# Rows of a head side by side in DRAM, early splits for the output projection, and two moved steps in an attention and MLP kernel

## The chip, the cores and the metric

The kernel runs on one core of one Trainium2 chip. The metric is the device time of one execution in microseconds (us); less is better. Engines are named as in the profile: PE is TensorE, with PEld for its weight loads, DVE is VectorE, ACT is ScalarE, POOL is GpSimd, and SP is SyncE, which here issues nearly all DMAs. An engine works through its instructions in program order; it stops at an instruction whose inputs or whose target buffer are not ready, and whatever stands behind that instruction stops with it.

## The reference

The reference is a transformer layer with layer normalization ahead of each half, in float32, on 2048 rows of 512:

```python
h  = x + A(layernorm(x), wqkv, wo)      # 32 heads of 16, softmax over 2048 keys
h2 = h + B(layernorm(h), w1, w2)        # silu(h @ w1) @ w2, 1792 wide
# A: q, k, v = split(x @ wqkv);  softmax(q @ k.T * 16 ** -0.5) @ v  for each head, then @ wo
# layernorm(x) = (x - mean) / sqrt(var + 1e-5)
```

The output is `h2`, 2048 x 512.

## The kernel before

**Precision.** A float32 operand of a large product is split in two: a high part (a rounded copy, type fp32r) and a low part (what is left, by a subtraction). A product takes three matmuls: high by high, low by high, high by low (`product`, with `mm` at L85). So a tile such as `oh`, `ol` (the high and low part of a 128-row piece of the attention's output `ot`) or `hth`, `htl` (of the turned, normalized rows) needs a copy and a subtraction before the matmuls that read it.

**Queries and keys.** `project_qk` makes 128 rows of q or k (8 heads of 16) for 512 positions, splits them in two 16-bit parts `sh` and `sl`, and stores them in the DRAM tiles `qd` and `kd`, which hold three sets of rows: for k the sets are high, low, high, for q high, high, low, so that one matmul over 48 rows gives all three partial products. `load_k` (L198) and `load_q` (L203) bring a head's 48 rows into the on-chip tiles `ks` and `qs`: 16 rows from each of three places in DRAM that are 512 rows apart. All DMAs stand in one queue on SP (`dma`, L105).

**Work by items.** The 32 heads and 4 blocks of 512 queries make 32 items of four heads each (item `i`: block `i // 8`). An item has 16 groups `c`, one for each 128 keys. In a group, PE makes four score tiles (`ps_s`), ACT takes their exponentials (`pt`, L99), and PE adds the values' products for an earlier group into the bank `pv`. The softmax needs a maximum for each query ahead of its scores: `maximum` (L218) is a matmul over the 48 rows into `ps_m` and a DVE reduction `mx` (L227). Sixty-four of these belong to an item; they are spread over the groups of an earlier item, mostly three or four to a group, by `one_max`, which counts them off. When an item's last maximum is found, `finish_max` folds them to `nm` (on DVE if urgent, on POOL if not) and splits that to `ns` on POOL, and `place_max` (L260) turns `ns` on PE (`ps_n`), copies it out (`mt`), and places it in `qs` by two DMAs.

**Around the end of a block.** An item's sums of exponentials go through DRAM (`sums`, `invert`, `spread`), and `divide` multiplies two items' rows of `ot` by the inverses `den` on POOL; each pair of items fills one of the four 128-column chunks of `ot`, so the last pair of a block fills chunk 3. This goes on while the next block's first item (`FIRSTS`: items 8, 16 and 24) has begun. In that item, at groups 0 to 3 the residual's rows are loaded into `hx`; at group `OUTPUT` = 9 `split_rows` splits row piece 0 on POOL (four chunks at once), at groups 10 to 12 pieces 1 to 3 (the high part on ACT, the low part on POOL), and at groups 10 to 15 `output(b, n)` runs for n = 0 to 5:

```python
project_rows(n)  -> ps_wo (12 matmuls), add_rows: ot <- ps_wo + hx     # n < 4
turn_rows(n - 2): hx turned on PE (ps_tr), hth on ACT, htl on DVE      # 1 < n < 6
found[n] = statistics(row piece n)  (st, mv on DVE, rs on POOL)        # n < 4
normalize(hx[n - 1])                                                   # 0 < n < 5
```

Then `finish_block` runs the MLP of that block (`mlp`): 14 steps `f`, each with the first product (12 matmuls into `ps_w` for f = 0, into the bank `pv` after that), a SiLU on ACT, and the second product of the step before. Bursts of maxima are woven in for the first two blocks and in part for the third. `marks` lists the groups before which an MLP runs; the last block's output and MLP are separate code at the end of the program (`finish_last`).

**Order.** The order on each engine is the order in which the program is written (`keep_in_program_order`). Steps are put off by a count of groups through an agenda (`soon`, `tick`). PSUM banks: in the attention four of kind `st` (scores, `ps_wo`, `ps_tr`, `ps_w`), three of kind `sm` (maxima, `ps_n`), one `pv`. The tiles `oh` and `ol` have two buffers each.

**First phase.** Before item 0 the rows of `x` are normalized and projected, block by block. Block 0's q and k for the first 8 heads are stored, and sixteen loads of 48 rows follow at once in SP's queue; the rows of `x` of block 3 (`load_x(3)`, 1 MB into a `ks` buffer) and the next stores stand behind them.

Of the kernel before, what the change touches and what calls it, by code (L numbers as in the profile page):

```python
# [11 lines left out]
F32R = mybir.dt.float32r  # L12
# [65 lines left out]
def attention_mlp_kernel(ctx: ExitStack, tc: tile.TileContext, x, wqkv, wo, w1, w2, out):  # L78
# [79 lines left out]
    qk_f = nc.scalar.alloc_register("qk_f")  # L158


    qd = dram.tile([3, D, S], F16, name="qd")
    kd = dram.tile([3, D, S], F16, name="kd")

    dn = dram.tile([H, 4, 512], F32, name="dn")
    dr = dram.tile([H, 4, 512], F32, name="dr")
# [29 lines left out]
        qs[i] = vpool.tile([P, 2, 512], F16, name=f"qs{i}")  # L195
    va = vpool.tile([P, KC, H, DH + 1], F32, name="va")

    def load_k(i, k, lo=0, n=S):  # L198
        a, j = HEADS[k]
        h = 4 * (i % 8) + 2 * a + j  # L200
        dma(ks[i % RING][64 * j:64 * j + 48, a, lo:lo + n], kd[:, h * DH:(h + 1) * DH, lo:lo + n])

    def load_q(i, k):  # L203
        a, j = HEADS[k]
        h = 4 * (i % 8) + 2 * a + j
        lo = i // 8 * 512
        dma(qs[i % RING][64 * j:64 * j + 48, a, :], qd[:, h * DH:(h + 1) * DH, lo:lo + 512])

    def fixed_rows(i):
        for j in range(2):  # L210
# [99 lines left out]
    def one_max(half=None, ps=None):  # L310

        i = next_item()
        if i == ITEMS:
            return
        if half is None:
            half = at["half"]
            at["half"] = 1 - half
        if at["blocks"]:

            i = min(range(2), key=lambda n: (todo[n, half] or todo[n, 1 - half] or [(n, KC)])[0][1])  # L320
        elif not todo[i, half] and 64 * (i + 2) <= at["ready"] and KC * i - at["next"] > 12:

            i += 1
        half = half if todo[i, half] else 1 - half
        at["done"] += 1
        found_all = maximum(*todo[i, half].pop(0), ps)

        finish_rest()
        if found_all:
            steps = due_at(i)  # L330
            if at["group"] is None:
                soon(steps, place_max, i)
                finish_max(i, False)
                return
            late.setdefault(at["step"] + steps, []).append(i)
            if steps == WAIT:
                unfinished.append(i)
                found_at["step"] = at["step"]
            else:
                finish_max(i, False)  # L340
# [34 lines left out]
    with ExitStack() as pa:  # L375
# [55 lines left out]
        def project_qk(b, n, beside={}, scale=False, kind="st"):  # L431

            g, key = divmod(n, 2)
            cols = slice(key * D + g * P, key * D + (g + 1) * P)
            ps = bank("ps_qk", kind)
            weave(product(ps, lambda c: wqk_h[:, c, cols], lambda c: wqk_l[:, c, cols],
                          lambda c: xth[b][:, c, :], lambda c: xtl[b][:, c, :], DC),
                  {k: n if callable(n) else (lambda n=n: burst(n)) for k, n in beside.items()})
            sh = xp.tile([P, 512], F16, name="sh")
            sl = xp.tile([P, 512], F16, name="sl", bufs=2)  # L440
            if scale:

                t = scaled[b]
                act("mul", t, ps, qk_s)
                act("copy", sh, t)
                pool("tensor_tensor", sl, t, sh, ALU.subtract)
            else:
                act("mul", sh, ps, qk_s)
                dve("scalar_tensor_tensor", sl, ps, qk_s, sh, op0=ALU.mult, op1=ALU.subtract)
            d = (kd if key else qd)[:, g * P:(g + 1) * P, b * 512:b * 512 + 512]  # L450
            hs, ls = (slice(0, 3, 2), 1) if key else (slice(0, 2), 2)
            dma(d[hs].rearrange("s d n -> d s n"), sh[:, None, :].to_broadcast([P, 2, 512]))
            dma(d[ls], sl)

        def project_v(b, t):
            ps = bank("ps_v")
# [296 lines left out]
                dve("tensor_copy", wh, w)  # L753
            low(wl, w, wh, engine)

    def split_rows(b, t):
        os[t] = [gp.tile([P, DC, P], F32R, name=name) for name in ("oh", "ol")]
        if t:
            act("copy", os[t][0], ot[b % 2][:, t])
        else:  # L760

            pool("tensor_copy", os[t][0], ot[b % 2][:, t])
        low(os[t][1], ot[b % 2][:, t], os[t][0], "pool")

    def split_wo(c, w):
        pool("tensor_copy", wo_h[:, c, :], w)
# [100 lines left out]
    def output(b, n):  # L867

        if n < 4:
            ps = bank("ps_wo")  # L870
            weave(project_rows(n, ps), {6: lambda: burst(3)} if n < MORE[b] else {})
            add_rows(b, n, ps)

        if 1 < n < 6:
            turn_rows(n - 2)
        if n < 4:
            found[n] = statistics(rows_of(b, n))
        if 0 < n < 5:
            normalize(hx[n - 1], rows_of(b, n - 1), *found.pop(n - 1))

    def finish_block(b, pending):

# [159 lines left out]
    for g in range(groups):  # L1042
        tick()
        i, c = divmod(g, KC)
        at["group"], at["next"] = None, g
        if g in marks:
            finish_block(i // 8 - 1, (g - 2, g - 1))
        if i + RING - 1 < ITEMS and 6 <= c < 14:
            (load_k if c % 2 else load_q)(i + RING - 1, c // 2 - 3)
        if g < DC:  # L1050
            w = gp.tile([P, 512], F32, tag="w", name="w", bufs=4)
            dma(w, wo[g * P:(g + 1) * P, :])
            soon(8, split_wo, g, w)
        if i in FIRSTS:
            b, n = i // 8 - 1, c - OUTPUT
            if c < 4:
                load_rows(b, c)
            if c in first_weights:
                load_weights(*first_weights[c])
            if n == 0:  # L1060
                split_rows(b, n)
            if c == 13:
                split_weights("w1", 0, "pool")
        if i == ITEMS - 1:
            if c < 4:
                load_rows(NB - 1, c)
                split_early(c)
            if c == 4:
                for f in range(3):
                    load_weights("w1", f)  # L1070
                load_weights("w2", 0)
                for f in range(2):
                    soon(5, split_weights, "w1", f, "dve", "dve")
        if g == 1:
            dve("memset", pv, 0.0)
        at["group"] = g
        n = maxima(g)

        half = 1 - HEADS[g % 2][1]
        j = next_item()  # L1080
        skip = int(n == 3 and j < ITEMS and len(todo[j, half]) < len(todo[j, 1 - half]))
        for m in range(4):
            k = m ^ (g % 2)
            if (g, k) not in pts:
                scores(g, k)
            if skip <= m < skip + n:
                one_max(1 - HEADS[k][1])
        if found_at["step"] < at["step"]:
            finish_rest()
        for j in late.pop(at["step"], ()):  # L1090

            place_max(j)
        if i in FIRSTS and OUTPUT < c < OUTPUT + 4:

            split_rows(i // 8 - 1, c - OUTPUT)
        if i in FIRSTS and c > OUTPUT:
            output(i // 8 - 1, c - OUTPUT - 1)
        if g - LAG >= 0 and not (g in marks or g - 1 in marks):
            values(g - LAG)
# [34 lines left out]
```

## Time and profile before

| what | value |
|---|---|
| median of 3 runs | 1682.99 us (1679.89 to 1685.68) |
| the profiled execution | 1681.44 us |
| its span | 1679.7 us |
| PE busy | 1657.4 us (99%), 10542 instructions |
| DVE busy | 1449.5 us (86%) |
| ACT busy | 1238.5 us (74%) |
| POOL busy | 397.5 us (24%) |
| granted PE clock, mean | 0.999 |
| longest groups | `mx` reductions on DVE 1258.8 us (x2009), exponentials on ACT 1011.6 us (x2048) |

The shares are means over unlike stages. A busy PE can still wait inside a matmul, and a matmul's end is modelled, so what PE loses is read from the idle time that the rows give in square brackets, with the instruction that ended it, and from the starts of neighbouring rows. In a row of the timeline the columns are the start, the length, the engine, the line and operation, what is written and read, the size and the count of instructions taken together.

### The profile page before, as it was taken

What the parts mean: (1) busy time and instruction counts of PE and PEld (TensorE: products, weight loads), DVE (VectorE), ACT (ScalarE), POOL (GpSimd) and SP (SyncE); (2) the same over time, 40 slices, a digit from 0 to 9 for tenths busy, and PEclk for the clock granted to TensorE, in tenths of its full rate; (3) what the DMA queues carried; (4) which work ended last, traced back from release to release, by engine and by line L of the source; (5) the groups of instructions that cost most, each with busy time, mean ns of one, the idle gap of its engine ahead of it and who ended that gap; (6) DMA issues with size and microseconds to landing.
All of it is one profiled execution on the core that took longest, in us unless ns stands there. A gap on an engine that the chain in (4) does not pass through costs nothing.

```text
span 1679.7 us, 28522 instructions
## 1 busy us (share of the span) xinstructions
PE 1657.4 (99%) x10542; PEld 648.8 (39%) x10542; DVE 1449.5 (86%) x2391; ACT 1238.5 (74%) x2438; POOL 397.5 (24%) x578
## 2 busy tenths in 40 slices
PE   9999999999999999999999999999999999999999
PEld 7666422222245532222245532222245542222387
DVE  7899999999978889999978889999978889997343
ACT  5323699999952279999953279999962379999743
POOL 5323411211244301211144311211135311211100
PEclk9999999999999999999999999999999999999999
DMA  5434311111222111111223111111222211100222
GB/s 181 115 92 145 115 44 36 40 49 36 62 64 85 58 49 32 37 52 37 60 62 89 60 50 31 37 47 40 62 63 79 69 50 32 35 12 21 64 76 81
DMA packets 100763, 102.82 MB, mean 61 GB/s; under 512 B 19092, under 2 KB 77524, under 8 KB 100624
## 3 DMA queue, kind: packets, MB, share of 16 engines
q1 hardware_dynamic: 100624, 101.01, 20.6%
q8 instruction: 82, 1.34, 0.3%
q14 instruction: 57, 0.47, 0.1%
HBM read 77.72 MB, written 17.29 MB: 57 GB/s over the span
## 4 chain that ended last, share of the span: by engine, by line
PE 86%; ACT 5%; DVE 4%; DMA 2%; POOL 1%; issue 1%; SPq 1%; DVEq 0%; POOLq 0%
PE pv L85 33%; PE ps_s L85 19%; PE ps_m L85 10%; PE ps_acc L85 10%; PE ps_qk L85 5%; ACT pt L99 5%; PE ps_wo L85 3%; PE ps_w L85 3%; PE ps_v L85 3%; DVE mx L227 2%; PE ps_tr L88 1%; SPq L105 1%; DMA ks<-in_A_x_dram 1%; POOL ri L92 1%; DVE pvs L102 0%
## 5 line engine op out<-in xcount | busy, mean ns | idle before, releaser
L227 DVE TENSOR_REDUCE mx<-ps_m 128x1 f32<-128x512 f32 x2009 | 1258.8, 684 | 89.0 <-PE ps_m L85 61.5
L99 ACT ACTIVATE pt<-ps_s 128x512 f32<-128x512 f32 x2048 | 1011.6, 609 | 36.1 <-PE ps_m L85 22.8
L85 PE MATMUL pv<-pt,va 128*17 128x512 f32 x4096 | 537.5, 598 | 1.7 <-DVE pv L102 0.5
L85 PE MATMUL ps_s<-qs,ks 64*128 64x512 f16 x2048 | 531.1, 379 | 3.1 <-ACT pt L99 1.7
L85 PE MATMUL ps_m<-ks,qs 48*128 48x512 f16 x2009 | 502.6, 380 | 3.3 <-DVE mx L227 3.3
L85 PEld LDWEIGHTS <-ks 64*128 64x128 f16 x2048 | 148.7, 95 | 546.7 <-issue 435.4
L92 POOL TENSOR_TENSOR ri<-rc,minus 128x16 f32<-128x16 f32 x31 | 90.7, 2924 | 339.3 <-DMA rc<-dn 339.3
L85 PEld LDWEIGHTS pv<-pt,va 128*17 128x17 f32 x4096 | 68.9, 95 | 218.0 <-issue 203.5
L85 PEld LDWEIGHTS <-qs 48*128 48x128 f16 x2048 | 117.7, 94 | 70.0 <-issue 63.9
L99 ACT CAST w2h<-w 128x512 fp32r<-128x512 f32 x56 | 34.7, 620 | 102.3 <-PE ps_acc L85 102.3
L99 ACT ACTIVATE g<-pv 128x512 f32<-128x512 f32 x39 | 23.3, 597 | 102.8 <-PE pv L85 102.8
L85 PE MATMUL ps_acc<-w2l,gh 128*128 128x512 f32 x224 | 92.9, 415 | 0.0
L85 PE MATMUL ps_acc<-w2h,gh 128*128 128x512 f32 x224 | 92.4, 413 | 0.0
L92 POOL TENSOR_TENSOR w2l<-w,w2h 128x512 fp32r<-128x512 f32 x42 | 53.8, 1282 | 153.4 <-ACT w2h L99 153.4
L85 PE MATMUL ps_acc<-w2h,gl 128*128 128x512 f32 x224 | 88.1, 393 | 0.0
L102 DVE TENSOR_TENSOR gl<-g,gh 128x512 fp32r<-128x512 f32 x53 | 37.2, 701 | 46.7 <-ACT gh L99 46.7
L99 ACT ACTIVATE ks<-ps_qk,qk_s 128x512 f32<-128x512 f32 x30 | 20.7, 690 | 72.3 <-PE ps_qk L85 65.7
L85 PE MATMUL pv<-htl,w1h 128*128 128x512 f32 x156 | 65.6, 420 | 0.0
L85 PE MATMUL pv<-hth,w1h 128*128 128x512 f32 x156 | 62.5, 401 | 0.0
L85 PE MATMUL pv<-hth,w1l 128*128 128x512 f32 x156 | 61.4, 393 | 0.0
L92 POOL TENSOR_TENSOR w1l<-w,w1h 128x512 fp32r<-128x512 f32 x42 | 54.3, 1292 | 10.8 <-ACT w1h L99 10.8
L92 POOL TENSOR_SCALAR nm<-nm 128x16 f32<-128x16 f32 x51 | 13.0, 255 | 183.7 <-DVE nm L237 180.3
(135 smaller groups left out, 1395.8 us busy)
## 6 DMA issues: line engine op xcount, KB each, us to landing
w<-in_B_w_dram SPq DMA_DIRECT2D x112, 256.0 KB
ks<-kd SPq DMA_DIRECT2D x120, 192.0 KB
qs<-qd SPq DMA_DIRECT2D x128, 48.0 KB
kd<-sh SPq DMA_DIRECT2D x16, 256.0 KB
qd<-sh SPq DMA_DIRECT2D x16, 256.0 KB
hx<-in_A_x_dram SPq DMA_DIRECT2D x16, 256.0 KB
ot<-pvs SPq DMA_DIRECT2D x124, 32.0 KB
den<-dr SPq DMA_DIRECT2D x124, 32.0 KB
```

Of the source, the lines that this page charges most:

```text
L85: tc.keep_in_program_order(nc.tensor.matmul(*a, **k))
L88: tc.keep_in_program_order(nc.tensor.transpose(*a))
L92: tc.keep_in_program_order(getattr(nc.gpsimd, op)(*a, **k))
L99: pin(getattr(nc.scalar, fn)(*a, **k))
L102: pin(getattr(nc.vector, fn)(*a, **k))
L105: pin(nc.sync.dma_start(*a))
L227: pin(nc.vector.tensor_reduce(mx[i][:, j, a, qt, kb:kb + 1], ps, axis=AX.X, op=ALU.max))
```

## The change

There are four edits.

1. **Layout.** `qd` and `kd` become `[D, 3, S]`: the three rows that belong to one of the 512 columns lie next to each other, and a head's 48 rows are adjacent. `rows_of_head` gives them as 48 rows; the loads' source pattern changes from three runs of 16 rows to one run of 48. The stores write the same 1 KB pieces, each to a place three rows further on than the last.
2. **The end of the maxima ahead of an MLP.** When an item's last maximum is found in the group just before a mark, `finish_max` is called at once with the urgent form and `place_max` is put on the agenda; before, the item went through the list of unfinished ones. This concerns the items finished there ahead of the first two blocks' MLPs.
3. **Early splits.** Row pieces 0 and 1 are split in two steps: chunks 0 to 2 at groups 3 and 4 and chunk 3 at group 9, all on POOL. The high part of piece 1 moves from ACT to POOL. Pieces 2 and 3 are split as before.
4. **Normalization.** In `output`, `normalize(hx[n - 1])` is written ahead of `turn_rows(n - 2)` and `statistics` of piece n.

```diff
-    qd = dram.tile([3, D, S], F16, name="qd")
-    kd = dram.tile([3, D, S], F16, name="kd")
+    qd = dram.tile([D, 3, S], F16, name="qd")
+    kd = dram.tile([D, 3, S], F16, name="kd")
...
+    def rows_of_head(t, h):
+        return t[h * DH:(h + 1) * DH].rearrange("d s n -> (d s) n")
+
     def load_k(i, k, lo=0, n=S):
...
-        dma(ks[i % RING][64 * j:64 * j + 48, a, lo:lo + n], kd[:, h * DH:(h + 1) * DH, lo:lo + n])
+        dma(ks[i % RING][64 * j:64 * j + 48, a, lo:lo + n], rows_of_head(kd, h)[:, lo:lo + n])
...
-        dma(qs[i % RING][64 * j:64 * j + 48, a, :], qd[:, h * DH:(h + 1) * DH, lo:lo + 512])
+        dma(qs[i % RING][64 * j:64 * j + 48, a, :], rows_of_head(qd, h)[:, lo:lo + 512])
...
         if found_all:
             steps = due_at(i)
-            if at["group"] is None:
+            g = at["group"]
+            if g is None or g + 1 in marks:
                 soon(steps, place_max, i)
-                finish_max(i, False)
+                finish_max(i, g is not None)
                 return
...
-            d = (kd if key else qd)[:, g * P:(g + 1) * P, b * 512:b * 512 + 512]
+            d = (kd if key else qd)[g * P:(g + 1) * P, :, b * 512:b * 512 + 512]
             hs, ls = (slice(0, 3, 2), 1) if key else (slice(0, 2), 2)
-            dma(d[hs].rearrange("s d n -> d s n"), sh[:, None, :].to_broadcast([P, 2, 512]))
-            dma(d[ls], sl)
+            dma(d[:, hs], sh[:, None, :].to_broadcast([P, 2, 512]))
+            dma(d[:, ls], sl)
...
-    def split_rows(b, t):
-        os[t] = [gp.tile([P, DC, P], F32R, name=name) for name in ("oh", "ol")]
-        if t:
-            act("copy", os[t][0], ot[b % 2][:, t])
+    def split_rows(b, t, chunks=slice(None)):
+        if chunks.start != DC - 1:
+            os[t] = [gp.tile([P, DC, P], F32R, name=name) for name in ("oh", "ol")]
+        (h, l), o = (x[:, chunks] for x in os[t]), ot[b % 2][:, t, chunks]
+        if t > 1:
+            act("copy", h, o)
         else:
 
-            pool("tensor_copy", os[t][0], ot[b % 2][:, t])
-        low(os[t][1], ot[b % 2][:, t], os[t][0], "pool")
+            pool("tensor_copy", h, o)
+        low(l, o, h, "pool")
...
             add_rows(b, n, ps)
+        if 0 < n < 5:
+            normalize(hx[n - 1], rows_of(b, n - 1), *found.pop(n - 1))
 
         if 1 < n < 6:
             turn_rows(n - 2)
         if n < 4:
             found[n] = statistics(rows_of(b, n))
-        if 0 < n < 5:
-            normalize(hx[n - 1], rows_of(b, n - 1), *found.pop(n - 1))
...
+            if c in (3, 4):
+
+                split_rows(b, c - 3, slice(0, DC - 1))
             if n == 0:
-                split_rows(b, n)
+                for t in range(2):
+                    split_rows(b, t, slice(DC - 1, DC))
...
-        if i in FIRSTS and OUTPUT < c < OUTPUT + 4:
+        if i in FIRSTS and OUTPUT + 1 < c < OUTPUT + 4:
 
             split_rows(i // 8 - 1, c - OUTPUT)
```

What stands on POOL at the end of block 0 before the change (`ri`, `rc`: the inversion of the last item's sums; `den`: the divide of chunk 3):

```order
L92 TENSOR_TENSOR ns<-nm,ns 128x2x8
L92 TENSOR_TENSOR ri<-rc,minus 128x16
L92 TENSOR_TENSOR rc<-rc,ri 128x16
L92 TENSOR_SCALAR rc<-rc 128x16
L92 TENSOR_TENSOR ri<-ri,rc 128x16
L92 TENSOR_TENSOR ot_2191<-ot_2191,den 128x4x128
L92 CAST oh<-ot_2191 128x512
L92 TENSOR_TENSOR ol<-ot_2191,oh 128x512 x2
```

The same place on POOL with the change:

```order
L92 CAST oh<-ot_2191 128x384
L92 TENSOR_TENSOR ol<-ot_2191,oh 128x384
L92 CAST oh<-ot_2191 128x384
L92 TENSOR_TENSOR ol<-ot_2191,oh 128x384
L92 TENSOR_TENSOR ri<-rc,minus 128x16
L92 TENSOR_TENSOR rc<-rc,ri 128x16
L92 TENSOR_SCALAR rc<-rc 128x16
L92 TENSOR_TENSOR ri<-ri,rc 128x16
L92 TENSOR_TENSOR ot_2191<-ot_2191,den 128x4x128
L92 CAST oh<-ot_2191 128x128
L92 TENSOR_TENSOR ol<-ot_2191,oh 128x128
L92 CAST oh<-ot_2191 128x128
```

Three quarters of two pieces now stand ahead of the inversion and the divide, and a quarter of each behind it; the second `ol` of 128 x 128 follows in the next row.

DVE in the output of block 0 before the change, at n = 2 (`mx` rows are maxima of the group):

```order
L102 TENSOR_TENSOR ot_2191<-ps_wo,hx 128x512
L102 TENSOR_TENSOR htl<-ps_tr,hth 128x4x128
L102 BN_STATS st<-ot_2191 128x6
L102 BN_AGGR mv<-st 128x2
L102 TENSOR_SCALAR hx<-ot_2191,mv,rs 128x512
L227 TENSOR_REDUCE mx<-ps_m 128x1 x3
```

And with the change (the reductions' line has become L231):

```order
L102 TENSOR_TENSOR ot_2191<-ps_wo,hx 128x512
L102 TENSOR_SCALAR hx<-ot_2191,mv,rs 128x512
L102 TENSOR_TENSOR htl<-ps_tr,hth 128x4x128
L102 BN_STATS st<-ot_2191 128x6
L102 BN_AGGR mv<-st 128x2
L231 TENSOR_REDUCE mx<-ps_m 128x1 x3
```

The normalization `hx` has moved ahead of the low part `htl` and the statistics.

PE at the head of step f = 1 of block 0's MLP before the change (`ps_n` turns the maxima's `ns`):

```order
L85 LDWEIGHTS qs_90
L85 MATMUL ps_m<-ks_89,qs_90 128x512
L88 LDWEIGHTS ns
L88 MATMUL ps_n<-ident_h,ns 32x128
L85 MATMUL pv<-hth,w1h 128x512
L85 MATMUL pv<-hth,w1l 128x512
```

And PE at the head of step f = 0 with the change, where `ps_n` now stands:

```order
L88 MATMUL ps_tr<-ident,hx 128x128 x4
L85 MATMUL pv<-pt,va 17x512 x12
L88 LDWEIGHTS ns
L88 MATMUL ps_n<-ident_h,ns 32x128
L85 MATMUL ps_w_6837<-hth,w1h 128x512
L85 MATMUL ps_w_6837<-hth,w1l 128x512
```

The transpose has moved from behind the maxima of step 0 to ahead of that step's first product; otherwise PE has the same instructions in the same order.

## The prediction

> **What bounds the kernel now.** I read the page first: PE is busy 99% of the span. That says little, since a waiting exponential also keeps PE's stream slow without an idle row. So I cut the program into its stages with the table of stretches. Columns: the stretch, its length, busy PE (and instructions), PEld, DVE, ACT, POOL, the granted clock, the DMA share, GB/s.
>
> ```profile
> 80.00:130.00 50.00, 49.75 (x237) 31.37 (x236) 48.57 (x81) 13.68 (x23) 13.53 (x19) 1.00 0.34 91
> 196.00:462.00 266.00, 265.46 (x2021) 59.27 (x2021) 254.04 (x414) 265.54 (x541) 49.22 (x80) 1.00 0.18 49
> 462.00:494.00 32.00, 29.91 (x178) 13.89 (x175) 25.40 (x46) 18.64 (x36) 11.80 (x18) 1.00 0.25 71
> 494.00:606.00 112.00, 111.07 (x488) 64.56 (x486) 94.95 (x154) 39.36 (x68) 43.40 (x50) 1.00 0.21 62
> ```
>
> In the attention (196 to 462) ACT is busy 265.54 of 266.00 us: the exponentials set the pace there, and nothing that the change does on PE, DVE or POOL in that stretch is worth anything as long as it doesn't make ACT wait. In the output stage (462 to 494) ACT is busy 18.64 of 32 and PE idles 2.09; in the MLP (494 to 606) PE sets the pace. In the first phase PE and DVE are both nearly full (49.75 and 48.57 of 50). A wait of PE in the output stage, which comes three times, or in the MLP or the first phase, delays everything behind it. Next I read what PE waits for, over the whole run (total us, times, longest).
>
> ```profile
> PE ps_m L85 <- DVE mx L227: 3.3, 7, 1.3
> PE ps_wo L85 <- POOL ol L92: 2.5, 3, 0.9
> PE ps_tr L88 <- DVE hx L102: 2.3, 3, 0.8
> PE ps_wo L85 <- POOL oh L92: 0.9, 1, 0.9
> ```
>
> Three of these four rows lie in the output stages, once or so in each of the three blocks, and name the steps that the change touches. They are all small: the whole change plays for some 10 us of 1681.
>
> **Early splits.** This is the timeline at the first output, and below it the rows of the second and third.
>
> ```profile
> 462.36 0.61 POOL L92 CAST oh<-ot 128x512 fp32r<-128x512 f32 x1
> 463.03 0.50 PE L85 MATMUL ps_wo<-wo_h,oh 128*128 128x512 f32 x1
> 463.06 1.27 POOL L92 TENSOR_TENSOR ol<-ot,oh 128x512 fp32r<-128x512 f32 x1
> 464.38 0.50 PE L85 MATMUL ps_wo<-wo_h,ol 128*128 128x512 f32 x1 [0.84 <-POOL ol L92]
> 464.72 0.40 PE L85 MATMUL ps_wo<-wo_l,oh 128*128 128x512 f32 x1
> 464.95 0.39 PE L85 MATMUL ps_wo<-wo_h,oh 128*128 128x512 f32 x1
> ```
>
> ```profile
> 838.77 5.99 ACT L99 ACTIVATE pt<-ps_s 128x512 f32<-128x512 f32 x12
> 844.25 0.50 PE L85 MATMUL ps_wo<-wo_h,oh 128*128 128x512 f32 x1 [0.94 <-POOL oh L92]
> 845.61 0.50 PE L85 MATMUL ps_wo<-wo_h,ol 128*128 128x512 f32 x1 [0.85 <-POOL ol L92]
> 1226.04 0.50 PE L85 MATMUL ps_wo<-wo_h,ol 128*128 128x512 f32 x1 [0.78 <-POOL ol L92]
> ```
>
> Matmuls of this product follow each other by 0.23 us (464.72 to 464.95). The second starts 464.38 - 463.03 = 1.35 after the first, so 1.12 is lost; in the second block 845.61 - 844.25 = 1.36, so 1.13; the third block's idle time is 0.06 less than the first's, so 1.05. Sum 3.3. With the change, chunk 0 of `oh` and `ol` is ready five groups before, and chunk 3 is needed by the tenth matmul, 9 x 0.23 = 2.1 us after the first. POOL's work between is a quarter of each: cover even if it cost the full 0.61 + 1.27 = 1.88. If that cover failed, the wait would come back at chunk 3.
>
> The first matmul also waited, in the second block 0.94 for `oh`. What is late next is its bank, which one of the group's four exponentials must free. Exponentials follow by (5.99 - 0.61) / 11 = 0.49 with 0.61 for one; this run of twelve ends at 844.76, so the first of its last four ends at 844.76 - 3 x 0.49 = 843.29, before PE is free for it at 844.25 - 0.94 = 843.31. So 0.9 goes. In the other blocks no such wait is recorded, and I count 0.1 for both. Early splits: 3.3 + 0.9 + 0.1 = **4.3** (3.3 if the second block's first wait finds another cause, 4.9 if the first matmul of each block gains 0.3 more).
>
> The early splits themselves lie in the attention, where POOL is busy 49.22 of 266 and ACT doesn't wait for POOL; in full size a piece takes 0.61 + 1.27 = 1.88, so two pieces take under 3.8 us of POOL in two groups of 4 x 0.49 = 1.96. The inversion of sums is queued behind them on POOL; it comes later in the program and the divide of chunk 3 later still, so a delay of some tenths there would show as a later `oh` at 462.36. I count nothing. Nor do I for piece 1's copy that leaves ACT, since ACT waits for PE in the output stage.
>
> **Normalization.** The rows of the first block at n = 2:
>
> ```profile
> 485.37 0.69 DVE L102 TENSOR_TENSOR htl<-ps_tr,hth 128x512 fp32r<-128x512 f32 x1 [0.30 <-ACT hth L99]
> 486.05 2.07 ACT L99 ACTIVATE pt<-ps_s 128x512 f32<-128x512 f32 x4 [0.72 <-PE ps_m L85]
> 486.79 0.52 DVE L102 TENSOR_SCALAR hx<-ot,mv,rs 128x512 f32<-128x512 f32 x1
> 487.45 0.63 PE L88 MATMUL ps_tr<-ident,hx 128*128 128x128 f32 x4 [0.78 <-DVE hx L102]
> 488.12 0.59 ACT L99 CAST hth<-ps_tr 128x512 fp32r<-128x512 f32 x1
> 489.42 1.57 ACT L99 ACTIVATE pt<-ps_s 128x512 f32<-128x512 f32 x3 [0.72 <-PE ps_m L85]
> 490.07 0.37 PE L85 MATMUL ps_s<-qs,ks 64*128 64x512 f16 x1 [0.25 <-ACT pt L99]
> 490.37 0.44 PE L88 MATMUL ps_tr<-ident,hx 128*128 128x128 f32 x2
> ```
>
> With `hx` ahead of `htl` and the statistics, it ends about 1.5 us sooner, and the wait of 0.78 goes. It doesn't all come through. What is late next is the bank of `ps_tr`: the first exponential of the group ends at 486.05 + 0.61 = 486.66, so the transposes start near 486.72, 0.73 sooner. PE then goes on to the next scores, whose exponentials start at 488.71 instead of 489.42: the copy `hth` keeps its place behind four exponentials, at 488.12 to 488.71, which is just in time. The scores at 490.07 wait for an exponential and so gain the same, but the next transposes (490.37) then wait for the bank of a later exponential, which I put at 489.87: 0.5 of the 0.7 is left. Three blocks: **1.5** (2.3 if the whole wait goes; 0 if the bank or the exponentials take all). The price is a later `htl`: it now stands behind 0.52 of `hx`, but DVE idled 0.30 ahead of it, so it is 0.2 later, and a group's length lies between it and the MLP. I count nothing for it.
>
> **The transpose of the maxima.** Before, PE at the heads of steps 1 and 0:
>
> ```profile
> 497.97 0.37 PE L85 MATMUL ps_m<-ks,qs 48*128 48x512 f16 x1 [0.20 <-DVE mx L227]
> 498.57 0.22 PE L88 MATMUL ps_n<-ident_h,ns 128*32 128x128 f16 x1 [0.23 <-DVE mx L227]
> 498.71 0.50 PE L85 MATMUL pv<-hth,w1h 128*128 128x512 f32 x1
> 492.81 0.22 POOL L92 TENSOR_TENSOR ns<-nm,ns 128x16 f16<-128x16 f32 x1
> 493.66 0.50 PE L85 MATMUL ps_w<-hth,w1h 128*128 128x512 f32 x1
> ```
>
> The transpose waited for a bank that a maximum's reduction frees. Without it, the product's first matmul would follow the maximum by 0.23, at 498.20 rather than 498.71: 0.5 gained. At its new place it costs its own slot, 498.71 - 498.57 = 0.14; its `ns` is ready at 493.03, before PE comes there at 493.66. So 0.35 in each of two blocks: **0.7** (0 to 1.0). The fold of the maxima on DVE comes one maximum earlier, and the copy `mt` and two DMAs on SP go with the transpose, one step sooner; nobody waits for them there. The third block has no such transpose.
>
> **Layout.** The trace doesn't show the new pattern, so this term is the least sure. The rows are SP's last of sixteen loads, the load of `x` behind them, DVE's wait for that, four maxima on PE and what follows, a wait for a load at the end of the first phase, a store-free stretch of the attention with only loads in flight, and a DMA whose two sides are spread otherwise.
>
> ```profile
> 43.34 0.67 SPq L105 DMA_DIRECT2D ks<-kd  x1
> 46.27 0.39 SPq L105 DMA_DIRECT2D ks<-in_A_x_dram  x1
> 54.48 0.69 DVE L102 BATCH_NORM_STATS2 st<-ks 128x6 f32<-128x512 f32 x1 [2.60 <-DMA ks<-in_A_x_dram]
> 55.95 0.39 PE L85 MATMUL ps_m<-ks,qs 48*128 48x512 f16 x1
> 57.61 0.37 PE L85 MATMUL ps_m<-ks,qs 48*128 48x512 f16 x1 [1.27 <-DVE mx L227]
> 59.11 1.08 PE L88 MATMUL ps_tr<-ident,ks 128*128 128x128 f32 x4
> 133.05 0.09 PEld L85 LDWEIGHTS <-qs 48*128 48x128 f16 x1 [1.38 <-DMA qs<-qd]
> 616.00:618.00 2.00, 2.00 (x18) 0.44 (x15) 1.93 (x4) 2.00 (x5) 0.00 (x0) 1.00 0.19 74
> 56.62 0.73 SPq L105 DMA_DIRECT2D qs<-fix_q  x1
> ```
>
> Loads alone keep a share of 0.19 of 16 engines busy: 3.0 engines, as many as the source has runs. So a load's packets queue on three engines, and the transfers of `x`, which need all, wait there too. The Trainium skill, page "DMA: Bandwidth & Descriptors", section "Why a DMA increments its semaphore by 16 and not by 1", says that the number of engines is the largest one up to 16 that divides the slowest dimension of both patterns: 3 before, which the 0.19 bears out, and 16 for 48 rows, which no run here shows yet. By that rule the sum below stands; with three engines as now it would be the first rival's. I take from the row alone that a pattern with 48 in the place of 3 spreads wider.
>
> DVE waits 2.60 for `x` at 54.48, and its reductions come late by as much: PE runs the four maxima from 55.95 to 59.11, 3.16 us, where four matmuls without a wait, 0.23 apart, would leave it after some 0.8. So up to 2.4 goes if `x` lands 2.6 sooner. SP issues it no sooner (46.27, after sixteen loads), only its way is free: I take the whole 2.4, since 8.2 us from issue to use is long for a transfer that shares three full engines. At 133.05 a weight load waits 1.38 for a load of queries, of which PE's last matmul (0.39) covers a part: PE loses about 1.0, and that load gets faster. The stores move the same pieces to places further apart; no row shows such a store, and the lower end allows for its cost. Sum **3.4** (0 to 4.5).
>
> **Sum.** 4.3 + 1.5 + 0.7 + 3.4 = 9.9. Against the profiled execution, 1681.4: **1671.5**. The median of the runs, 1682.99, lies 1.6 higher, by which it would be 1673.1; I keep the first and let the range hold the second. By upper ends 4.9 + 2.3 + 1.0 + 4.5 = 12.7: 1668.7.
>
> **The rivals.**
> - *The loads gain nothing on the path.* Either the layout does not spread the packets, or DVE, full for 48.57 of 50 us behind that place, eats what PE gains. Against: DVE too starts 2.6 sooner. Left is 4.3 + 1.5 + 0.7 = 6.5: 1675. Chance 0.20.
> - *The output stages keep their length.* Exponentials and banks pace the groups there too: each row with 0.72 at ACT's start shows ACT waiting for PE and not the other way, which speaks against. Only 3.4 is left: 1678. Chance 0.10.
> - *Slower: SP's price for a load.* A load holds SP's queue 0.67 us now, a fill with a 16-row pattern 0.73. If 48 separate rows cost more to write out, the sixteen loads ahead of `x` delay it by 16 times the surplus. At twice the price that is 16 x 0.67 = 10.7 later at DVE's wait; the layout's 3.4 is lost, and the total is 1681.4 - 6.5 + 10.7 = 1685.6. It decides from a surplus of 6.5 / 16 = 0.41 on. The 0.73 is far below that. Chance 0.07.
> - *Nothing moves*: the gains of all parts are taken up before the next attention's first exponential, 1681. Against: ACT idles in all these stages, so nothing there takes them up. Chance 0.05.
>
> **How the numbers follow.** The forecast has 0.58. A measurement can tell about 0.3%, 5 us, from no change. Faster by more: the forecast, and 0.18 of the first rival's 0.20 (6.5 is near the bound) = 0.76. Within: 0.02 + 0.10 + 0.05 = 0.17. Slower: 0.07. The range goes from the upper ends less the runs' scatter (1682.99 - 1679.89 = 2.9), 1665.8, to the second rival from the median's side, 1678.0 + 1.6 = 1679.6; it leaves out the slower case, that of nothing, and a part of the others' scatter.
>
> **What would show it.** Right: no wait of `ps_wo` for POOL, the stretch of 32.00 us at the output about 2 shorter; `ps_tr` waiting for an exponential and not for `hx`; `ps_n` in PE's row ahead of the first `ps_w`; the share of 0.19 in load-only stretches spread over more engines, a shorter wait at DVE for `x`, SP's load still near 0.7. Wrong: a load above 1.0 on SP, a wait for `x` that is still there, a new wait of PE for `htl` at the MLP's head, or a wait for `oh` at chunk 3.

## The result and the profile after

| | before | after |
|---|---|---|
| median of 6 runs each | 1681.08 us | 1670.37 us |
| lowest to highest | 1679.89 to 1685.68 | 1670.20 to 1670.89 |
| span of the profiled execution | 1679.7 | 1668.4 |

The ratio is 0.9932, with a 95% interval of 0.992 to 0.9945. By medians the change is worth 10.7 us, by the two profiled spans 11.3. The scatter fell too, from 5.8 us to 0.7. Of the kernels tested below, four had one run each of 2356 to 8553 us, which the ratios and ranges leave out and the medians count as one run of twelve. Where the time came from is read from the starts of the same instructions in both traces, since PE has the same instructions in the same order but for the place of one transpose in each of the first two blocks:

| instruction | before | after | difference | new here |
|---|---|---|---|---|
| `ps_v` behind DVE's wait for `x` | 62.54 | 58.50 | -4.04 | 4.04 |
| `ps_m` behind the load of queries | 133.05 | 128.15 | -4.90 | 0.86 |
| a `pv` shortly ahead of the first output | 455.00 | 450.35 | -4.65 | -0.25 |
| block 1: third matmul of `ps_wo` | 464.72 | 458.91 | -5.81 | 1.16 |
| block 1: `ps_tr` at n = 3 | 490.37 | 484.02 | -6.35 | 0.54 |
| block 1: `pv` at the head of step 1 | 498.71 | 491.97 | -6.74 | 0.39 |
| block 2: third matmul of `ps_wo` | 845.94 | 837.24 | -8.70 | 1.96 |
| block 2: `ps_tr` at n = 3 | 871.58 | 862.35 | -9.23 | 0.53 |
| block 2: `pv` at the head of step 1 | 879.92 | 870.31 | -9.61 | 0.38 |
| block 3: third matmul of `ps_wo` | 1226.37 | 1215.71 | -10.66 | 1.05 |
| block 3: `ps_tr` at n = 3 | 1250.55 | 1239.35 | -11.20 | 0.54 |

So in this pair of profiles the layout gave 4.65, the early splits 1.16 + 1.96 + 1.05 = 4.17, the normalization 1.61 and the transpose of the maxima 0.77: 11.2 of the 11.3. The waits of PE after the change, whole run:

```profile
PE ps_s L85 <- ACT pt L99: 1.6, 5, 0.5
PE ps_i L88 <- POOL ident masks.py:199: 1.5, 1, 1.5
PE ps_m L85 <- DVE mx L231: 0.7, 3, 0.3
PE ps_n L88 <- DVE mx L231: 0.6, 4, 0.2
```

The three rows that the prediction was made from, `ps_wo` for `ol` and `oh` and `ps_tr` for `hx`, are gone, and `ps_m` for `mx` fell from 3.3 to 0.7. At the first output, timeline after:

```profile
458.37 0.47 PE L85 MATMUL ps_wo<-wo_h,oh 128*128 128x512 f32 x1
458.68 0.40 PE L85 MATMUL ps_wo<-wo_h,ol 128*128 128x512 f32 x1
459.42 0.46 POOL L92 TENSOR_TENSOR ol<-ot,oh 128x128 fp32r<-128x128 f32 x1
480.88 0.42 PEld L88 LDWEIGHTS ps_tr<-ident,hx 128*128 128x128 f32 x4 [0.53 <-ACT pt L99]
484.02 0.42 PEld L88 LDWEIGHTS ps_tr<-ident,hx 128*128 128x128 f32 x4 [0.98 <-ACT pt L99]
487.19 0.22 PE L88 MATMUL ps_n<-ident_h,ns 128*32 128x128 f16 x1
487.34 0.51 PE L85 MATMUL ps_w<-hth,w1h 128*128 128x512 f32 x1
```

The second matmul follows the first by 0.31, and chunk 3 of `ol` is ready at 459.42 + 0.46 = 459.88, ahead of the tenth matmul, which starts at 461.26 behind three maxima. The transposes now wait for an exponential, that is, for their bank. `ps_n` takes 0.15 ahead of the MLP's first matmul. In the first phase, SP's last load, the load of `x`, and what waited for it (timeline after):

```profile
38.89 0.43 SPq L105 DMA_DIRECT2D ks<-kd  x1
40.39 0.41 SPq L105 DMA_DIRECT2D ks<-in_A_x_dram  x1
51.93 0.68 DVE L102 BATCH_NORM_STATS2 st<-ks 128x6 f32<-128x512 f32 x1
56.08 0.61 PE L85 MATMUL ps_m<-ks,qs 48*128 48x512 f16 x4
```

A load holds SP for 0.43 and not for 0.67, so `x` is issued 5.9 us sooner; DVE's wait of 2.60 is gone, and the four maxima stand in one row. The loads at the start of an attention, in stretches of 1 us after:

```profile
606.00:607.00 1.00, 1.00 (x12) 0.21 (x6) 1.00 (x2) 1.00 (x3) 0.00 (x0) 1.00 0.97 224
608.00:609.00 1.00, 1.00 (x12) 0.21 (x6) 0.98 (x2) 1.00 (x3) 0.00 (x0) 1.00 0.42 81
609.00:610.00 1.00, 1.00 (x9) 0.23 (x9) 0.95 (x2) 1.00 (x4) 0.00 (x0) 1.00 0.04 12
```

The DMA share there is 0.97 and soon 0.04, where it was 0.19 before: all sixteen engines for a short time. This is what the rule from the Trainium skill, page "DMA: Bandwidth & Descriptors", named in the prediction gives for 48 rows.

One thing in the trace of before had not been seen ahead of the result. PE's matmuls behind the wait for `x` followed each other by 0.42 and not by 0.23 (stretches of 2 us, before; the clock is the third value from the right):

```profile
56.00:58.00 2.00, 0.71 (x3) 0.14 (x3) 1.77 (x4) 0.00 (x0) 1.92 (x4) 1.00 0.20 67
58.00:60.00 2.00, 1.57 (x7) 0.99 (x7) 1.97 (x5) 1.31 (x2) 0.50 (x1) 0.80 0.68 125
60.00:62.00 2.00, 2.00 (x6) 1.62 (x6) 1.97 (x6) 0.59 (x1) 1.58 (x4) 0.50 0.83 122
62.00:64.00 2.00, 2.00 (x8) 1.33 (x7) 2.00 (x4) 0.00 (x0) 2.00 (x3) 0.85 0.84 99
```

The granted clock fell to 0.50 behind a stretch in which PE was busy 0.71 of 2 us. The wait took 2.5 us, and the slow matmuls behind it took another 1.5.

### The profile page after: what moved, and what is told of

Its sections match the earlier page's. It is cut to its first block, busy times and chain, and to the rows that moved or that the text cites. A ratio compares the mean times of both kernels' runs of the same rounds, so it can differ in the third digit from the quotient of the medians.

```text
span 1668.4 us, 28544 instructions
## 1 busy us (share of the span) xinstructions
PE 1655.0 (99%) x10542; PEld 648.1 (39%) x10542; DVE 1448.6 (87%) x2391; ACT 1236.4 (74%) x2435; POOL 399.0 (24%) x593
## 4 chain that ended last, share of the span: by engine, by line
PE 89%; ACT 5%; DVE 4%; issue 1%; DMA 1%; POOL 0%; SPq 0%; DVEq 0%; POOLq 0%
PE pv L85 34%; PE ps_s L85 20%; PE ps_m L85 11%; PE ps_acc L85 10%; PE ps_qk L85 5%; ACT pt L99 5%; PE ps_wo L85 3%; PE ps_w L85 3%; PE ps_v L85 3%; DVE mx L231 2%; PE ps_tr L88 1%; DVE pvs L102 0%; PE ps_n L88 0%; DVE st L102 0%; SPq L105 0%
## 5 line engine op out<-in xcount | busy, mean ns | idle before, releaser
L231 DVE TENSOR_REDUCE mx<-ps_m 128x1 f32<-128x512 f32 x2009 | 1258.8, 684 | 83.3 <-PE ps_m L85 55.7
L92 POOL TENSOR_TENSOR mx<-mx 128x32 f32<-128x32 f32 x38 | 9.5, 250 | 199.1 <-DVE mx L231 197.5
```

Of the source, the lines that this page charges most:

```text
L92: tc.keep_in_program_order(getattr(nc.gpsimd, op)(*a, **k))
L231: pin(nc.vector.tensor_reduce(mx[i][:, j, a, qt, kb:kb + 1], ps, axis=AX.X, op=ALU.max))
```

## The experiments

The theory was that the parts act at separate places and add up, and that a wait can cost more than its length by the clock. The rivals were that the parts help or hide each other, and that a wait costs its length. All ratios are to the kernel before, run on the same chip. The three groups of kernels below ran on three different chips, so a kernel of one group is compared with one of another by its ratio.

### Each part alone

The edits are the four parts of the diff above, each put into the kernel before.

> The layout alone (part 1), nothing else changed. Theory (the parts act at separate places and add up): the whole gain of the first phase comes from here, so the first exponential starts 4.6 us earlier than in the kernel before and the time is 4.7 us less (ratio 0.9972); the output stages keep all their waits (ps_wo for POOL 3.4 in all, ps_tr for hx 2.3). Rival (the parts help each other, so that a part alone is worth less): under 3.5 us less.

> The early splits alone (part 3). Theory: 4.1 us less (1.1, 2.0 and 1.0 in the three blocks), all of it at the first and second matmul of ps_wo; the first phase as before. Rival (the gain at ps_wo is taken back by the later wait of ps_tr for hx, which stays here): 2 us less or none, with a longer wait of ps_tr for hx than 2.3 in all.

> The normalization's place alone (part 4). Theory: ps_tr no longer waits for hx, 0.75 gained at n = 2 of each block and 0.2 given back at n = 3 by a wait for an exponential: 1.6 us less in all (ratio 0.999). Rival (ACT's exponentials pace the group, so that nothing is left of it at the MLP): 0 to 0.3 us less.

> The maxima's transpose ahead of the MLP alone (part 2). Theory: 0.4 us at the head of step 1 of the first two MLPs, 0.8 us less in all, too little for the times but plain in the trace. Rival (at its new place the transpose costs what it saves, or the MLP's second step waits for DVE instead): 0.

| part alone | median | ratio (95%) | runs, lowest to highest |
|---|---|---|---|
| before | 1681.64 | | 1678.62 to 1686.52 |
| layout | 1676.63 | 0.9970 (0.9959 to 0.9982) | 1676.23 to 1677.22 |
| early splits | 1675.71 | 0.9969 (0.9956 to 0.9981) | 1674.55 to 1681.37 |
| normalization | 1680.19 | 0.9997 (0.9986 to 1.0008) | 1677.95 to 1688.58 |
| maxima's transpose | 1680.52 | 0.9991 (0.9980 to 1.0003) | 1678.44 to 1684.26 |

The four sum to 0.30 + 0.31 + 0.03 + 0.09 = 0.73%, against 0.68% for the whole: within the intervals, each some 0.12% to either side, they add up. With the layout alone the first exponential starts at 180.91 and not at 185.11, 4.2 sooner where 4.6 was expected, and the output keeps its waits, 3.4 for POOL and 2.3 for `hx`. With the early splits alone the waits for POOL are gone and that for `hx` is still 2.3, so the rival there fell. The last two are too small for the times alone; their traces show the same steps as the whole change: with the normalization alone `ps_tr` at n = 2 comes 0.75 sooner and 0.21 is lost again at n = 3, and with the transpose alone the head of step 1 comes 0.38 sooner.

The three kernels without the layout have the first phase of the kernel before, instruction for instruction, and yet DVE's wait for `x` differs (timelines of the early splits, of the normalization and of the transpose alone):

```profile
52.72 0.69 DVE L102 BATCH_NORM_STATS2 st<-ks 128x6 f32<-128x512 f32 x1 [0.82 <-DMA ks<-in_A_x_dram]
```
```profile
53.72 0.70 DVE L102 BATCH_NORM_STATS2 st<-ks 128x6 f32<-128x512 f32 x1 [1.55 <-DMA ks<-in_A_x_dram]
```
```profile
53.44 0.69 DVE L102 BATCH_NORM_STATS2 st<-ks 128x6 f32<-128x512 f32 x1 [0.63 <-DMA ks<-in_A_x_dram]
```

0.82, 1.55 and 0.63, against 2.60 in the profiled execution before: the wait is a matter of the execution, and the 4.65 of the table above is one draw of it. In these three the first exponential starts at 182.40, 183.38 and 183.24, against 185.11 before and 180.47 with the whole change: measured from them, the layout's first phase is worth 1.9 to 2.9. The 5.0 that the layout alone gains by medians seems to hold more than this phase. In none of these three did the clock fall there. It fell elsewhere, in the kernel with the transpose alone, at the second block's output (stretches of 2 us):

```profile
842.00:844.00 2.00, 1.03 (x2) 0.69 (x3) 0.35 (x1) 0.99 (x3) 1.92 (x3) 0.82 0.24 65
844.00:846.00 2.00, 2.00 (x7) 1.11 (x6) 0.00 (x0) 0.00 (x0) 0.64 (x1) 0.50 0.54 168
```

That wait for `oh` and `ol` is in the kernel before as well, where the clock stayed at 1.00. So what the early splits take away also cost more than its length in some executions, which may be why they alone gave 5.9 by medians and 4.2 by the starts. The mean granted clock of each run points the same way. Of the 27 runs of the kernel before in this group, eight have 0.997 or 0.998 and took 1682.0 to 1686.5; the other nineteen have 0.999 or 1.000 and took 1678.6 to 1683.5. All runs of the layout alone and of the early splits alone have 0.999 or 1.000.

### What in the layout counts

In the kernel before, only the order of a load's rows: 16 runs of 3, DRAM as it was (and the same for q):

```diff
-        dma(ks[i % RING][64 * j:64 * j + 48, a, lo:lo + n], kd[:, h * DH:(h + 1) * DH, lo:lo + n])
+        dma(ks[i % RING][64 * j:64 * j + 48, a, lo:lo + n], kd[:, h * DH:(h + 1) * DH, lo:lo + n].rearrange("s d n -> d s n"))
```

> The kernel before with its old layout (three sets 512 rows apart); only the order in which a load names its 48 rows is changed, so that its source has 16 runs of 3 rows and not 3 runs of 16 (q and k alike, so the products are the same). Theory A (what counts is over how many DMA engines a load is spread): all of the layout's 4.7 us comes, although no rows are adjacent, and the share of load-only stretches is spread wider. Theory B (what counts is SP's time for a load, 0.67 before and 0.42 after): SP still takes about 0.67, since the pattern still has three levels, and x is issued as late as before: under 1.5 us less. Theory C (what counts is that the rows are adjacent): nothing.

In the changed kernel, the adjacent rows named in 3 runs:

```diff
-        return t[h * DH:(h + 1) * DH].rearrange("d s n -> (d s) n")
+        return t[h * DH:(h + 1) * DH].rearrange("d s n -> s d n")
```

> The changed kernel, but each load names its 48 adjacent rows in 3 runs of 16 rows (every third row). Theory A (engines): the load goes over 3 engines again, and the layout's 4.7 us are lost: about 1675. Theory B (SP's time): SP takes 0.67 again, and most of the 4.7 us is lost as well. Theory C (adjacent rows): nothing is lost, 1670.4.

In the kernel before, `x` ahead of the second eight loads:

```diff
                         for i in range(2):
+                            if b == 0 and i == 1:
+                                load_x(3)
...
-                if b == 1 and n == 0:
-                    load_x(3)
```

> The kernel before, with the 1 MB load of x for the last block issued behind the first eight of the sixteen loads instead of behind all and two stores; layout as before. It takes the wait of DVE for x away by an earlier issue alone. Theory (the wait for x is worth 3.6 us: 2.5 of waiting and about 1.1 of a lower clock after it): 3 to 3.6 us less by the time of the next projections, if the second eight loads, now later, do not hold the first maxima up. Rival (DVE's own work paces this stretch): under 1 us less.

| kernel | median | ratio (95%) | SP for a load | DVE's wait for `x` | `ps_m` behind the load of queries |
|---|---|---|---|---|---|
| before | 1681.31 | | 0.67 | 2.60 | 133.05 |
| before, 16 runs of 3 | 1679.31 | 0.9983 (0.9973 to 0.9994) | 0.59 | none | 128.06 |
| changed, 3 runs of 16 | 1673.04 | 0.9949 (0.9930 to 0.9967) | 0.68 | 0.28 | 129.74 |
| before, `x` sooner | 1680.40 | 0.9993 (0.9980 to 1.0006) | 0.67 | none | |

The load-only stretches of the two kernels, first with 16 runs, then with 3 runs of adjacent rows:

```profile
609.00:610.00 1.00, 1.00 (x11) 0.13 (x8) 1.00 (x3) 1.00 (x3) 0.00 (x0) 1.00 0.80 183
613.00:614.00 1.00, 1.00 (x9) 0.13 (x8) 1.00 (x3) 1.00 (x3) 0.00 (x0) 1.00 0.19 68
```

The 16 runs reach a share of 0.80, the 3 runs stay at the 0.19 of the kernel before. With 16 runs and no adjacent rows the first phase is that of the changed kernel, 133.05 to 128.06: adjacency is not needed there. With adjacent rows in 3 runs, the kernel is slower than the changed one by 0.17% in the ratios, 2.9 us, though the intervals overlap; its span is 1.8 longer. That is less than the 4.7 of theory A. PE waits for the queries again:

```profile
129.74 0.39 PE L85 MATMUL ps_m<-ks,qs 48*128 48x512 f16 x1 [0.97 <-DMA qs<-qd]
```

So the spread over the engines is what the layout does for that wait (theory A; B and C fall there: SP's time with 16 runs was nearer the old, 0.59, and the whole gain came). For the wait for `x` these profiles do not tell the spread from an earlier issue. A load of `x` issued 7.7 us sooner behind slow loads, at 38.54, had none, and PE stood 3.6 us earlier from there to 175 us; but 3 runs with an issue at 44.80 had only 0.28, and the wait moves by some 2 us without any edit. In the median of the kernel with `x` sooner little of the 3.6 is left, 0.9 us, with an interval that holds zero. Five of its twelve runs have a mean clock of 0.996 to 0.998, so a part may have gone to a lower clock elsewhere; where is not shown.

The kernel with 16 runs has the first phase's gain, but its median is 2.0 less than before and not the 4.7 of theory A: by the ratios 2.2 slower than the layout alone, with intervals that overlap, and by the two spans 2.2 as well. In the profile the outputs hold the difference (timeline and stretches):

```profile
458.43 0.49 PE L85 MATMUL ps_wo<-wo_h,oh 128*128 128x512 f32 x1 [0.41 <-POOL oh L92]
459.78 0.52 PE L85 MATMUL ps_wo<-wo_h,ol 128*128 128x512 f32 x1 [0.85 <-POOL ol L92]
460.95 0.63 PE L85 MATMUL ps_wo<-wo_h,ol 128*128 128x512 f32 x1
```
```profile
460.00:462.00 2.00, 2.00 (x7) 1.12 (x7) 0.00 (x0) 0.00 (x0) 1.27 (x1) 0.53 1.06 217
842.00:844.00 2.00, 1.89 (x5) 1.28 (x5) 0.00 (x0) 0.16 (x1) 1.33 (x2) 0.61 1.08 221
```

Behind waits of 0.41 and 0.85 the clock fell to 0.53, in the second block, behind 0.54 and 0.85, to 0.61 and then 0.54. Against the layout alone PE loses 1.6 from the first output's start to its end and 1.5 in the second: more than the 2.2 between the two spans. With the layout alone PE waited there for `ol` only, 0.79, but in the second block as long as in the kernel before, and the clock stayed. Why it fell here is open.

### Whether the clock is the cause

> The kernel before, with six transposes of the identity (work of no use) on PE behind the first of the four maxima that wait for DVE and x, so that PE is busy in a part of its wait; the wait itself stays. Theory (a wait of that length lowers PE's granted clock, which costs another 1.1 to 1.4 us after it): granted clock near 1.0 in the 5 us behind the wait, and about 1 us less in the trace. Rival (the matmuls behind the wait are slow for another reason, such as the DMA load of that stretch): the clock row and the pitch of 0.42 stay, 0 us.

The edit puts `idle(6)` behind the first of four maxima:

```diff
+                    if b == 2 and n == 0:
+                        burst(1)
+                        idle(6)
+                        n_max -= 1
```

It tells nothing on this, for two reasons that the timeline shows:

```profile
52.97 0.39 PE L85 MATMUL ps_m<-ks,qs 48*128 48x512 f16 x1
53.29 0.87 PE L88 MATMUL ps_i<-ident 128*128 128x128 f32 x6
57.58 0.61 PE L85 MATMUL ps_m<-ks,qs 48*128 48x512 f16 x4
```

The transposes stand one group of maxima too early: the maxima in which PE waited before, from 55.95 on, are those at 57.58 here. And `x` came in time, so there was no wait to fill. The median was 1684.09 (ratio 1.0017, 1.0003 to 1.003), 2.8 more than before, which six transposes of 0.87 together do not explain; where the runs lose it is open. One such loss shows in the trace, a wait for the rows that `place_max` puts in `qs`, at the start of an item:

```profile
442.70 0.60 PE L85 MATMUL ps_s<-qs,ks 64*128 64x512 f16 x1 [2.63 <-DMA qs<-mt]
```
```profile
442.00:444.00 2.00, 1.29 (x7) 0.43 (x7) 0.62 (x2) 0.66 (x2) 0.00 (x0) 0.51 0.05 19
446.00:448.00 2.00, 2.00 (x11) 0.43 (x7) 0.96 (x2) 1.00 (x3) 0.00 (x0) 0.50 0.00 0
```

A wait of 2.63, and a clock of 0.50 to 448. This wait, too, is a matter of the execution. The early splits and the normalization alone had this wait too (0.9 and 0.3); the layout alone and the changed kernel, none.

So the clock was put to the test at the outputs: part 3 undone; then the first piece's low part made twice, which makes the wait longer; then with ten transposes of the identity (`no_use`, in a bank of the maxima's kind) in that wait.

```diff
-        low(os[t][1], ot[b % 2][:, t], os[t][0], "pool")
+        for _ in range(1 if t else 2):
+            low(os[t][1], ot[b % 2][:, t], os[t][0], "pool")
...
+            if n == 0:
+                inserts[1] = lambda: no_use(10)
```

> The changed kernel with part 3 undone (the splits late again). Theory (a wait of PE costs its own length, and beyond some length a lower granted clock behind it, in some of the executions): 4.1 us more than the changed kernel, 1674.5, or more where the clock falls behind a wait; the runs scatter by more than the changed kernel's 0.7 us. Rival (a wait costs its length and nothing else): 1674.5 with the scatter of the changed kernel.

> The same with the first piece's low part subtracted twice on POOL, so that PE's wait for it at the start of each output grows by 1.28, to about 2.4; nothing else is longer. Theory (clock): each block then loses the 1.28 and another 1.4 to 1.5 by a granted clock of about one half for some 3 us: 3 x 2.7 = 8.2 more than the kernel with late splits, about 1682.7. Rival (a wait costs its length): 3 x 1.28 = 3.8 more, about 1678.3, clock 1.00 behind the wait.

> The same with ten transposes of the identity (no use) on PE between the first two matmuls of the output, 2.2 us of PE's time that lies in the wait of 2.4. The wait for POOL ends when it did. Theory (clock): PE is kept busy, the clock stays at 1.00, and the time is that of the rival above, about 1678.3. Rival (the matmuls behind such a wait are slow for another reason, or the transposes cost what they save): the time of the kernel with the doubled wait or more.

| kernel | median | ratio to before (95%) |
|---|---|---|
| part 3 undone | 1676.30 | 0.9966 (0.9953 to 0.9979) |
| and the wait made longer | 1683.41 | 1.0004 (0.9993 to 1.0015) |
| and PE kept busy in it | 1679.76 | 0.9982 (0.9972 to 0.9991) |

The longer wait costs 7.1 with PE idle in it and 3.5 with PE busy in a part of it, where POOL's added work is 3 x 1.27 = 3.8. The rows of the first output, with PE idle:

```profile
461.75 0.79 PE L85 MATMUL ps_wo<-wo_h,ol 128*128 128x512 f32 x1 [2.19 <-POOL ol L92]
462.34 0.63 PE L85 MATMUL ps_wo<-wo_l,oh 128*128 128x512 f32 x1
462.77 0.63 PE L85 MATMUL ps_wo<-wo_h,oh 128*128 128x512 f32 x1
```
```profile
460.00:462.00 2.00, 0.25 (x1) 0.25 (x2) 0.00 (x0) 0.03 (x1) 1.92 (x3) 0.65 1.17 228
462.00:464.00 2.00, 2.00 (x5) 1.24 (x5) 0.00 (x0) 0.00 (x0) 0.93 (x1) 0.50 1.16 236
```

And with PE busy:

```profile
459.96 1.25 PE L88 MATMUL ps_i<-ident 128*128 128x128 f32 x10
462.32 0.50 PE L85 MATMUL ps_wo<-wo_h,ol 128*128 128x512 f32 x1 [1.11 <-POOL ol L92]
462.66 0.39 PE L85 MATMUL ps_wo<-wo_l,oh 128*128 128x512 f32 x1
462.89 0.40 PE L85 MATMUL ps_wo<-wo_h,oh 128*128 128x512 f32 x1
```
```profile
460.00:462.00 2.00, 1.21 (x11) 0.97 (x9) 0.00 (x0) 0.32 (x1) 1.92 (x2) 1.00 1.20 231
462.00:464.00 2.00, 1.68 (x8) 0.97 (x8) 0.00 (x0) 0.00 (x0) 1.51 (x2) 1.00 1.18 234
```

The second matmul starts 2.69 and 2.70 behind the first (459.06 and 459.62), so the wait for POOL is the same, and so is the DMA share, 1.17 and 1.20; only with PE idle does the clock fall, and the matmuls follow by 0.43 and not by 0.23. The transposes take 1.25 of the 2.36 from their start to the second matmul, and that was enough. The profile of the kernel with PE idle is its slowest run but for the one left out, so its rows show the upper end; but the mean clock is 0.995 to 0.998 in all eleven of its runs and 0.999 or 1.000 in all eleven with PE busy. That a wait of PE can cost more than its length, by the clock, is shown. It does not always: the profile with part 3 undone has the longest waits in the second block,

```profile
838.85 0.49 PE L85 MATMUL ps_wo<-wo_h,oh 128*128 128x512 f32 x1 [1.43 <-POOL oh L92]
840.20 0.50 PE L85 MATMUL ps_wo<-wo_h,ol 128*128 128x512 f32 x1 [0.85 <-POOL ol L92]
```
```profile
840.00:842.00 2.00, 1.80 (x8) 0.97 (x8) 0.01 (x1) 0.00 (x0) 1.39 (x2) 1.00 1.14 207
```

and the clock stays at 1.00.

Undoing part 3 costs 5.7 by the ratios and widens the runs from 0.7 to 3.6 (1674.46 to 1678.04): more than the 4.1 of waits, as the theory has it. The two runs with a mean clock of 1.000 took 1674.46 and 1674.57, the waits' price and no more; the other five, at 0.998 and 0.999, took 1676.09 to 1678.04. The profile is that of 1674.57, and its waits of 4.3 in all account for the 4.4 by which its span exceeds the changed kernel's:

```profile
PE ps_wo L85 <- POOL ol L92: 2.5, 3, 0.9
PE ps_wo L85 <- POOL oh L92: 1.8, 2, 1.4
```

The first wait, for `oh` behind the divide, is 1.8 in two blocks here and was 0.9 before: it depends on when `den` arrives, and the early splits leave only a quarter of a split behind it.

### A further step

The changed kernel's transposes wait for a bank of the scores; here they take one of the maxima's:

```diff
-        turn(hx.pop(t), hth[:, :, t * P:(t + 1) * P], htl[:, :, t * P:(t + 1) * P])
+        turn(hx.pop(t), hth[:, :, t * P:(t + 1) * P], htl[:, :, t * P:(t + 1) * P], "sm")
```

> The changed kernel with the transposes of the output's rows in a bank of the maxima's kind and not of the scores'. In the changed kernel these transposes wait for an exponential to free their bank. Theory: that wait goes, 0.2 at n = 2 and 0.25 at n = 3 of each block, 1.3 us less: 1669.1. Rival (the maxima then wait for their banks, which DVE frees): the same time or up to 1 us more.

The median is 1672.20 (0.9939, 0.9925 to 0.9953), with runs from 1672.0 to 1672.7. By the ratios that is 1.2 slower than the changed kernel, with intervals that overlap, and by the spans 1.6. The theory fell, and the rival held:

```profile
PE ps_tr L88 <- DVE mx L231: 2.4, 3, 0.8
481.61 0.66 PE L88 MATMUL ps_tr<-ident,hx 128*128 128x128 f32 x4 [0.81 <-DVE mx L231]
```

At n = 2 the wait for an exponential turned into one of 0.81 for a maximum's reduction.

## Why the prediction was right

- **The whole**: 1671.5 forecast, 1670.37 measured; 9.9 less forecast, 11.2 found in the traces and 10.7 by medians.
- **Early splits**, 4.3: 4.17 in the traces, by blocks 1.16, 1.96 and 1.05 where 1.2, 2.0 and 1.1 were worked out. That the second block's first wait would go as well, because the bank is free, held. Left out was the clock: behind these very waits it fell in two of the other kernels.
- **Normalization**, 1.5: 1.61. What was named as next, the bank, was next: 0.75 came at n = 2 and 0.2 was given back at n = 3.
- **The maxima's transpose**, 0.7: 0.77. Both sides of this small sum were off and nearly cancelled: at the head of step 1 0.44 came and not 0.5, and at the new place the first product starts only 0.03 later, since PE had a gap of 0.11 there, and not 0.14.
- **Layout**, 3.4: 4.65, above the term's own upper end of 4.5. This is the term that was mis-sized. The wait of DVE for `x` was priced at 2.4 of PE's time, the length of the wait; PE lost 4.04 there, 2.5 by the wait and 1.5 because the clock behind it fell to 0.50. Of this 0.42 was lost again at the next maxima (`ps_m` at 60.67), where PE waits for DVE's reductions. The load of queries gave 1.28 where 1.0 was counted, and 0.25 was lost again before the first output. And the step "SP issues it no sooner" failed: SP's time for a load went down by 0.24 to 0.43, where "still near 0.7" was named as a sign of being right, and `x` was issued 5.9 us sooner.
- **The rivals.** That the loads gain nothing fell with the layout alone (5.0 by medians), that the output stages keep their length fell with the early splits alone. The slower one, SP's price, had its sign wrong.

The size of the layout's term is in part luck. It was read from a profile with a wait of 2.60 for `x`; from one of the three others with the same first phase the same reading would have found 0.63 to 1.55 and a term smaller by 1 to 2. The output's terms do not hang on this: their waits are there in every profile without the edits.

The prediction had the scatter only as a margin of its range, with no cause. The kernel before, with those that share its code, lost 0.3 to 2.6 us in several waits whose length differs from run to run (`x`, the queries, `qs` behind `mt`, `den`), and in part of the runs a slower clock behind them. The profile of the changed kernel has none of the first three, and its 6 runs lie within 0.7 us at a mean clock of 1.000.

## What to carry to other kernels

Price a wait of PE by its length and then look at the granted clock and the pitch of the matmuls behind it; a wait at the start of a dependent chain can cost nearly twice its length (7.1 for 3.8 of added waits here), and filling half of it with matmuls of no use took that second price away. Look at how many DMA engines a small, frequent load keeps busy (its share in a stretch where it runs alone, times 16), and name its rows so that it is spread: 3 runs kept a share of 0.19 here, 16 runs reached 0.80 and 48 rows 0.97. A wait for a DMA in one profile is one draw: profiles of kernels that share the code show how far it moves, and the mean clock of every run shows whether the profiled one is typical.

## What the runs showed of the hardware

- The clock fell to 0.50 behind one wait of PE of 2.63 us and behind 0.98 and 2.19 with one matmul between, and to 0.53 behind 0.41 and 0.85. It stayed at 1.00 behind 0.94 and 0.85 in the kernel before, behind 1.43 and 0.85 with part 3 undone, and behind 2.17 and 1.11 with a matmul and ten transposes between (third block of the kernel with PE kept busy). So the length of a wait did not decide it alone. In the third block of the kernel with the longer wait the slow matmuls began only 1.5 us after the wait of 2.19 had ended (1230.51 to 1232.01). The Trainium skill, page "TensorE: Matmul & The Clock Gate", section "Part 1: The HAM clock gate (the "warmup" mystery)", gives half the clock after at least one idle window of about 3.4 us, in windows that run freely. The 0.50 agrees, and free windows would fit that equal waits ended differently; but no wait here was 3.4 us long, so the measured bound is lower.
- SP's time for one DMA of 48 rows was 0.42 with a pattern of two levels, 0.59 with 16 runs of 3 and 0.67 to 0.68 with 3 runs of 16.
